# A repeated load taken out, and VectorE's attention steps made smaller and moved inside a pair of blocks, in a fused attention and gated feed-forward kernel

## The chip, the cores and the metric

The kernel runs on one core of a Trainium2 chip. The metric is device time in microseconds (us) of one execution. The time of a kernel is given as the median of its runs. A ratio is the mean time of one kernel's fast runs over that of the other's of the same rounds, so it is not quite the ratio of the medians that stand beside it.

## The reference, cut to what matters

```python
# batch 8, heads 8, seq 576, head_dim 64; all float32
kv  = einsum('bhsd,bhse->bhde', k, v)
out = einsum('bhsd,bhde->bhse', q, kv)
x   = out / sqrt(mean(out*out, -1) + 1e-6) * g_norm      # then (B*S, H*D) = (4608, 512)
gate, val = sigmoid(x @ w_gate), x @ w_val               # 512 -> 1536
return (gate * val) @ w_out                              # 1536 -> 512
```

## The kernel before

The tokens are done in nine chunks of 512. The first chunk is done plainly, beside the loading and converting of the weights and the attention of the first two batches. Chunks 1 to 8 use products with fewer multiplications: a first layer of six pairs of blocks, seven pairs of products each (p1, p6, p2, p7, p5, p4, p3), then a second layer. The attention of batch c + 1 is fed into chunk c, for c from 1 to 6, as a list of small steps. One step is taken from the list after each pair of products. Such a place is called a slot: 42 in the first layer, 28 in the second.

The first two batches, as pairs of heads n = 0 to 7 (NE = 8):

```python
def q_out():                                     # step of pair n
    nc.scalar.copy(out=qT, in_=d["q"])           # after TensorE's transposes of q, line 266
    load_q(n + 4 if n + 4 < NE else n + 2)       # n = 2 asks for q of 6; n = 4 asks for it again
```

The steps of a later batch (NQ = 3; cuts marked):

```python
def kv_copies(i):
    for r in range(NQ):
        nc.vector.tensor_copy(out=kvq[...], in_=kvs[...])
def turn(n):
    for e in range(2):
        nc.vector.transpose(qTs[...], pairs[n]["q"][...])
    load_q(n + 2)
...
fill.extend([turn(n0), turn(n0 + 1)] + [idle] * (0 if early else 5) + [kv_mm, kv_out])   # kv_mm in slot 7
fill.extend([kv_copies(i) for i in range(4)])
fill.extend(two_pairs(n0))     # u_mm (TensorE, reads kvq and qTs), square, sums, root, norms, x_mm, x_out
fill.extend([turn(n0 + 2), turn(n0 + 3)])
fill.extend(two_pairs(n0 + 2))
```

Of the kernel before, what the change touches and what calls it, by code (L numbers as in the profile page):

```python
# [20 lines left out]
def kernel(  # L21
# [11 lines left out]
    nc = tc.nc  # L33

    B, H, S, HD = q.shape
# [4 lines left out]
    NJ = 6  # L40
    NP = S // NJ
# [8 lines left out]
    QB = 32  # L50
    NQ = NP // QB
    QC = QB * NJ
    NC = HD // QB
# [22 lines left out]
    NE = 2 * NHP  # L76
    pairs = {n: {} for n in range(B * NHP)}
# [10 lines left out]
    def load_q(n):  # L88
        if n >= B * NHP:
            return  # L90
        b, h0 = n // NHP, 2 * (n % NHP)
        if n < NE:
            t = first.tile([NP, NJ, 2, HD], FP32, tag="q", name="q")
            for e in range(2):
                nc.sync.dma_start(out=t[:, :, e, :], in_=q[b, h0 + e].rearrange("(p j) d -> p j d", j=NJ))
        else:
            t = sb.tile([NP, 2, NJ * HD], FP32, tag="q", name="q")
            nc.sync.dma_start(out=t, in_=q[b, h0:h0 + 2].rearrange("h (p j) d -> p h (j d)", j=NJ))
        pairs[n]["q"] = t
# [127 lines left out]
    qTs = const.tile([P, 2, 2 * NJ * HD], FP32, name="qTs")  # L227
# [16 lines left out]
    def attention(n, at_ps):  # L244

        b, m = divmod(n, NHP)
        d = {}
        kv = kvs[:, m]

        def kv_mm():  # L250
            d["kv"] = ps = at_ps("kv")
            for j in range(NJ):
                js = slice(HD * j, HD * j + HD)
                for e in range(2):
                    nc.tensor.matmul(ps[HD * e:HD * e + HD, 0, 0:HD], pairs[n]["k"][:, e, js], pairs[n]["v"][:, e, js],  # L255
                                     start=(j == 0), stop=(j == NJ - 1))

        def kv_out():
            nc.vector.tensor_copy(out=kv, in_=d["kv"][:, 0, 0:HD])
            load_kv(n + 4)  # L260

        def q_mm():
            d["q"] = ps = at_ps("q")
            for j in range(NJ):
                c0 = NP * (j % JH)
                nc.tensor.transpose(ps[:, j // JH, c0:c0 + NP], pairs[n]["q"][:, j].rearrange("p e d -> p (e d)"),  # L266
                                    ident[0:NP, 0:NP])

        def q_out():
            d["qT"] = qTs[:, n % 2, 0:S]  # L270
            nc.scalar.copy(out=d["qT"].rearrange("p (i n) -> p i n", i=2), in_=d["q"][:, :, 0:JH * NP])
            load_q(n + 4 if n + 4 < NE else n + 2)

        def u_mm():


            ps = at_ps("u")
            d["u"] = ps[:, :, 0:NU * HD]
            for i in range(2 * NU):
                t0 = min(PH * i, S - PH)  # L280
                r = PH * (i % 2)
                for e in range(2):
                    es = slice(HD * e, HD * e + HD)
                    nc.tensor.matmul(d["u"][r:r + PH, e, HD * (i // 2):HD * (i // 2) + HD],  # L284
                                     d["qT"][es, t0:t0 + PH], kv[es], start=True, stop=True)

        def u_square():
            d["sq"] = sqs[:, NU * P * (n % 2):NU * P * (n % 2 + 1)].rearrange("p (e c) -> p e c", e=2)
            nc.scalar.activation(out=d["sq"], in_=d["u"], func=AF.Square)

        def u_sum():
            d["ms"] = sb.tile([P, 2, NU], FP32, tag="ms", name="ms")
            nc.vector.tensor_reduce(out=d["ms"].rearrange("p e i -> p (e i)"),
                                    in_=d["sq"].rearrange("p e (i d) -> p (e i) d", d=HD), axis=AX.X, op=ALU.add)

        def u_root():
            nc.scalar.activation(out=d["ms"], in_=d["ms"], func=AF.Sqrt, bias=eps, scale=1.0 / HD)

        def u_norm():

            nc.vector.reciprocal(d["ms"], d["ms"])
            d["xn"] = d["sq"].rearrange("p e c -> p (e c)")
            nc.vector.tensor_tensor(out=d["xn"].rearrange("p (i e d) -> p e i d", e=2, d=HD),
                                    in0=d["u"].rearrange("p e (i d) -> p e i d", d=HD),
                                    in1=d["ms"].unsqueeze(3).to_broadcast([P, 2, NU, HD]), op=ALU.mult)

        def x_mm():
            d["x"] = ps = at_ps("x")
            for i in range(NU):
                bank, c0 = divmod(P * i, UX)  # L310
                nc.tensor.transpose(ps[:, bank, c0:c0 + P], d["xn"][:, P * i:P * i + P], ident)  # L311

        def x_out():

            s0 = 0
            while s0 < S:
                c, o = divmod(S * b + s0, G)
                i, r = divmod(s0, UX)
                n_ = min(G - o, (UX if i == 0 else S - UX) - r)
                nc.scalar.activation(out=chunk(c)[:, m, o:o + n_], in_=d["x"][:, i, r:r + n_], func=AF.Copy, scale=g_col)  # L320
                s0 += n_

        return [kv_mm, kv_out, q_mm, q_out, u_mm, u_square, u_sum, u_root, u_norm, x_mm, x_out]


    fill = deque()

    def slot():
        if fill:
            fill.popleft()()  # L330

    def feed(b):

        early = b == 2
# [18 lines left out]
        def kv_out():  # L353
            nc.vector.tensor_copy(out=kvs, in_=d["kv"][:, :, 0:HD])

        def kv_copies(i):
            for r in range(NQ):
                nc.vector.tensor_copy(out=kvq[QB * r:QB * r + QB, :, i], in_=kvs[QB * i:QB * i + QB])  # L358

        def turn(n):  # L360

            for e in range(2):
                w_ = NJ * HD
                nc.vector.transpose(qTs[0:NP, n % 2, w_ * e:w_ * e + w_],
                                    pairs[n]["q"][:, e].rearrange("p (j i c) -> p i j c", i=NC, c=QB))
            load_q(n + 2)

        def two_pairs(n0):

# [26 lines left out]
            def u_sum(i):  # L396
                nc.vector.tensor_reduce(out=ms[:, :, units[i]], in_=by_head(sq)[:, :, units[i]], axis=AX.X, op=ALU.add)
# [4 lines left out]
            def u_norm(i):  # L402
                if i == 0:
                    nc.vector.reciprocal(ms, ms)
                m_ = ms[:, :, units[i]]
                nc.vector.tensor_tensor(out=by_head(sq)[:, :, units[i]], in0=by_head(d["u"])[:, :, units[i]],
                                        in1=m_.unsqueeze(3).to_broadcast([P, NQ, NJ // 2, HD]), op=ALU.mult)
# [7 lines left out]
            def x_out(which):  # L415

                m, s0 = (n0 + which) % NHP, 0
                while s0 < S:
                    c, o = divmod(S * b + s0, G)
                    r, c0 = divmod(s0, QC)  # L420
                    n_ = min(G - o, S - s0) // QC if c0 == 0 else 0
                    w_ = QC if n_ else min(G - o, QC - c0)
                    n_ = max(n_, 1)
                    nc.scalar.activation(out=chunk(c)[:, m, o:o + n_ * w_].rearrange("p (r c) -> p r c", r=n_),
                                         in_=d["x"][:, r:r + n_, QC * which + c0:QC * which + c0 + w_], func=AF.Copy,
                                         scale=g_col)
                    s0 += n_ * w_

            return [u_mm, u_square, lambda: u_sum(0), lambda: u_sum(1), u_root, lambda: u_norm(0), lambda: u_norm(1),
                    idle, x_mm, lambda: x_out(0), lambda: x_out(1)]  # L430

        def idle():
            pass

        n0 = NHP * b
        fill.extend([lambda: turn(n0), lambda: turn(n0 + 1)] + [idle] * (0 if early else 5) + [kv_mm, kv_out])
        fill.extend([lambda i=i: kv_copies(i) for i in range(2 * NC)])
        fill.extend(two_pairs(n0))
        fill.extend([lambda: turn(n0 + 2), lambda: turn(n0 + 3)])
        fill.extend(two_pairs(n0 + 2))  # L440

    def flush():
        while fill:
# [84 lines left out]
    def plain(c, f, ps):  # L528

        blk = Plain(c, f, ps)  # L530
        for at in range(2 * NMT):
            blk.mm(*divmod(at, NMT))
            if at in (0, 2) and late:
# [8 lines left out]
    steps = {"KV": KV, "KVO": KV_OUT, "Q": Q, "QO": Q_OUT, "U": U, "SQ": U_SQUARE, "SUM": U_SUM, "ROOT": U_ROOT,  # L542
             "NORM": U_NORM, "X": X, "XO": X_OUT}
# [16 lines left out]
    for token in order.split():  # L560
        name = token.rstrip("0123456789.")
        n = [int(i) for i in token[len(name):].split(".")]
# [70 lines left out]
    NF2 = NFT // 2  # L633
# [192 lines left out]

    for c in range(1, NG):
        if c + 1 < B:
            feed(c + 1)
        if c == 1:  # L830

            steps = list(fill)
            fill.clear()
            while w2_sums or steps:
                fill.append(w2_sums.popleft() if w2_sums and len(fill) % 7 in (2, 3) else steps.pop(0))
        first_layer_fast(c)
        sums_of(c + 1)
        second_layer_fast(c)
        flush()
# [30 lines left out]
```

## Time and profile before

| | before |
|---|---|
| median of 3 runs | 1116.73 us (1112.47 to 1117.07) |
| span of the profiled run | 1114.4 us |
| TensorE busy | 1091.4 us, 98% |
| VectorE busy | 617.2 us, 55% |
| granted TensorE clock, mean | 0.992 |

The table is where the argument starts: TensorE is busy nearly all the time, so a gain can only come out of its waits and out of stretches in which it runs slower than it could. The prediction shows the views in which both are seen: the table of waits, the chain of work that ended last, and the timeline. In a line of the chain the columns are start, length, and what ran. In a line of the timeline there follow the tile written and read, sizes, the count, and in brackets the idle time before it with what ended it.

### The profile page before, as it was taken

To read this page: it belongs to the slowest core of one execution; us is meant where nothing else is said; L and a number is where in the kernel's file an instruction comes from. 1 tells how busy PE (TensorE), PEld (TensorE's weight loads), DVE (VectorE), ACT (ScalarE), POOL (GpSimd) and SP (SyncE) were. 2 spreads that over 40 slices of the span, in tenths; PEclk is the share of its full clock that TensorE was granted. 3 is DMA by queue.
4 is the path that set the end of the run, shared out by engine and by line. 5 is a ranking of instruction groups with operands and counts; after the bars stand their busy time and mean duration, and the time that the engine had idled before them with its cause. 6 is when DMAs were issued, how large, how long until landed. Compare 5 with 4: busy or idle time off the path is not lost.

```text
span 1114.4 us, 18252 instructions
## 1 busy us (share of the span) xinstructions
PE 1091.4 (98%) x7334; PEld 902.0 (81%) x7334; DVE 617.2 (55%) x1219; ACT 267.3 (24%) x545; POOL 285.3 (26%) x390
## 2 busy tenths in 40 slices
PE   9799999999999999999999999999999999999997
PEld 8444447888888888888888888888888888888886
DVE  4497775773367527771676347642766155515641
ACT  4463322331124101330133013310232011101110
POOL 0000022441234204440334124420344044404500
PEclk9899999999999999999999999999999999999999
DMA  9944712000400022000400040003100000000001
GB/s 266 221 151 151 236 38 60 1 23 19 125 2 22 1 81 65 22 2 19 126 1 23 18 122 7 22 2 107 38 2 1 22 17 1 1 28 11 1 1 38
DMA packets 59657, 58.41 MB, mean 52 GB/s; under 512 B 20916, under 2 KB 53556, under 8 KB 59572
## 3 DMA queue, kind: packets, MB, share of 16 engines
q1 hardware_dynamic: 59412, 57.23, 17.6%
q8 instruction: 59, 0.97, 0.4%
q14 instruction: 26, 0.21, 0.1%
q10 hardware_dynamic: 160, 0.00, 0.0%
HBM read 47.78 MB, written 9.44 MB: 51 GB/s over the span
## 4 chain that ended last, share of the span: by engine, by line
PE 94%; DVE 4%; issue 1%; DMA 1%; SPq 0%; ACT 0%; POOL 0%; DVEq 0%; POOLq 0%
PE mm L669 49%; PE mm L755 26%; PE mm L516 7%; PE mm L613 4%; DVE kvq L358 2%; PE at L388 2%; PE at L344 1%; PE at L413 1%; PE mm L594 1%; PE at L516 1%; DMA q<-in_q_dram 1%; PE two L255 1%; PE two L284 0%; PE two L311 0%; PE two L266 0%
## 5 line engine op out<-in xcount | busy, mean ns | idle before, releaser
L656 POOL TENSOR_TENSOR tw<-gv 128x256 f32<-128x256 f32 x192 | 138.8, 733 | 775.2 <-PE mm L669 612.0
L669 PE MATMUL mm<-xT,gv 128*128 128x256 f32 x768 | 184.8, 384 | 0.0
L669 PE MATMUL mm<-xT,tw 128*128 128x256 f32 x768 | 181.6, 379 | 0.5 <-DVE gv L683 0.5
L669 PE MATMUL mm<-sx,tw 128*128 128x256 f32 x768 | 182.0, 380 | 0.0
L669 PEld LDWEIGHTS mm<-xT,gv 128*128 128x128 f32 x768 | 146.6, 192 | 21.2 <-issue 0.5
L669 PEld LDWEIGHTS mm<-xT,tw 128*128 128x128 f32 x768 | 145.8, 190 | 20.6 <-issue 0.8
L669 PEld LDWEIGHTS mm<-sx,tw 128*128 128x128 f32 x768 | 145.2, 190 | 19.7
L656 POOL TENSOR_TENSOR tw<-gv,tw 128x256 f32<-128x256 f32 x192 | 151.7, 811 | 0.2
L669 PE MATMUL mm<-sx,gv 128*128 128x256 f32 x384 | 91.3, 381 | 0.0
L701 ACT ACTIVATE sg<-sg 128x256 f32<-128x256 f32 x96 | 39.5, 417 | 206.7 <-DVE sg L700 206.3
L755 PE MATMUL mm<-w,s 128*128 128x256 f32 (+1 forms) x408 | 88.3, 367 | 0.0
L755 PE MATMUL mm<-w,gv 128*128 128x256 f32 x384 | 88.1, 379 | 0.0
L755 PE MATMUL mm<-t2w,gv 128*128 128x256 f32 x384 | 88.1, 379 | 0.0
L708 DVE TENSOR_TENSOR gv<-gv,sg 128x512 f32<-128x512 f32 x96 | 88.1, 956 | 0.0
L691 DVE TENSOR_TENSOR gv<-mm,sg 128x256 f32<-128x256 f32 x96 | 40.6, 424 | 81.6 <-PE mm L669 81.6
L677 ACT COPY sg<-mm 128x256 f32<-128x256 f32 x96 | 35.7, 372 | 201.6 <-PE mm L669 183.6
L755 PEld LDWEIGHTS mm<-w,s 128*128 128x128 f32 x408 | 74.1, 190 | 9.4
L755 PEld LDWEIGHTS mm<-w,gv 128*128 128x128 f32 x384 | 72.9, 190 | 9.9
L755 PEld LDWEIGHTS mm<-t2w,gv 128*128 128x128 f32 x384 | 72.9, 190 | 9.9
L669 PEld LDWEIGHTS mm<-sx,gv 128*128 128x128 f32 x384 | 72.5, 190 | 10.0
L516 PE MATMUL mm<-xT,gv 128*128 128x512 f32 x176 | 79.5, 606 | 0.0
L705 DVE TENSOR_TENSOR gv<-mm,gv 128x256 f32<-128x256 f32 x96 | 40.2, 423 | 44.8 <-PE mm L669 44.5
(99 smaller groups left out, 1040.8 us busy)
## 6 DMA issues: line engine op xcount, KB each, us to landing
q<-in_q_dram SPq DMA_DIRECT2D x24, 288.0 KB
st<-in_moe_w_gate_dram SPq DMA_DIRECT2D x12, 512.0 KB
st<-in_moe_w_val_dram SPq DMA_DIRECT2D x12, 512.0 KB
st<-in_moe_w_out_dram SPq DMA_DIRECT2D x12, 512.0 KB
kv<-in_k_dram SPq DMA_DIRECT2D x24, 256.0 KB
kv<-in_v_dram SPq DMA_DIRECT2D x24, 256.0 KB
out_dram<-sg SPq DMA_DIRECT2D x17, 256.0 KB
out_dram<-sg SPq DMA_DIRECT2D x25, 128.0 KB
```

The lines of the kernel that those rows point to most:

```text
L358: nc.vector.tensor_copy(out=kvq[QB * r:QB * r + QB, :, i], in_=kvs[QB * i:QB * i + QB])
L388: nc.tensor.matmul(u[PH * half:PH * half + PH, r, P * s + HD * e:P * s + HD * e + HD], qTs[QB * r:QB * r + QB, (n0 + which) % 2, c:c + PH] ...
L516: nc.tensor.matmul(self.ps[i], w[("wg", "wv")[i], self.f][:, m, :], xT[self.c][:, m, :], start=(m == 0), stop=(m == NMT - 1), skip_group_c ...
L613: nc.tensor.matmul(ps[t], gv[0, f][:, P * t:P * t + P], w["wo", f], start=(f == 0), stop=(f == NFT - 1), skip_group_check=True)
L656: nc.gpsimd.tensor_tensor(out=tw[f, i], in0=b[in0], in1=b[in1] if isinstance(in1, tuple) else tw[f, in1], op=ALU.subtract)
L669: nc.tensor.matmul(ps, wt[:, m, :], xs[:, m, :], start=(new and m == 0), stop=(m == NK - 1), skip_group_check=True)
L677: nc.scalar.copy(out=d["sg"][:, h2], in_=pa)
L691: tt(out=d["h"][:, h2], in0=d["pb"], in1=d["sg"][:, h2], op=ALU.add)
L701: nc.scalar.activation(out=d["sg"][:, h2], in_=d["sg"][:, h2], func=AF.Sigmoid)
L705: tt(out=d["h"][:, h1], in0=d["pc"], in1=d["h"][:, h1], op=ALU.add)
L708: tt(out=d["h"], in0=d["h"], in1=d["sg"], op=ALU.mult)
L755: nc.tensor.matmul(ps, hs(f), ws[:, f, :], start=(new and f == 0), stop=(f == NF2 - 1), skip_group_check=True)
```

## The change

Two things are intended. The second load of q for pairs 6 and 7 is dropped. And VectorE's steps for attention are halved and put only into those slots of a pair of blocks in which VectorE has room. The core of the diff, with cuts marked:

```diff
-            load_q(n + 4 if n + 4 < NE else n + 2)
+            for i in (n + 4,) if n + 4 < NE else (n + 2,) if n + 2 >= NE else ():
+                load_q(i)
...
-        def kv_copies(i):
-            for r in range(NQ):
+        def kv_copies(i, rs):
+            for r in rs:
...
-        fill.extend([lambda: turn(n0), lambda: turn(n0 + 1)] + [idle] * (0 if early else 5) + [kv_mm, kv_out])
-        fill.extend([lambda i=i: kv_copies(i) for i in range(2 * NC)])
-        fill.extend(two_pairs(n0))
-        ...
+        steps = turns_of(n0) + turns_of(n0 + 1)
+        if b > 2:
+            steps += [(PE, idle)] * (7 - len(steps))
+        steps += [(PE, kv_mm), (DVE, kv_out)]
+        for i in range(2 * NC):
+            for rs in ((0, 1), (2,)):
+                steps.append((DVE, lambda i=i, rs=rs: kv_copies(i, rs)))
+        steps += u0 + turns_of(n0 + 2) + x0 + turns_of(n0 + 3) + u1 + [(PE, idle)] * 2 + x1
...
+    def spread(steps, at):
+        n = 0
+        for engine, step in steps:
+            while engine == DVE and n < 7 * NF2 and n % 7 not in at:
+                fill.append(idle)
+                n += 1
+            fill.append(step)
+            n += 1
...
+            spread(steps, (1, 2, 3, 4, 5) if c == 1 else (2, 3, 4, 5))
```

More of the change, by code (lines that the diff above doesn't have):

```diff
@@ L330, in slot @@
             fill.popleft()()
+    PE, DVE, ACT = range(3)
     def feed(b):
@@ L354, in kv_out, with turn @@
             nc.vector.tensor_copy(out=kvs, in_=d["kv"][:, :, 0:HD])
-        def kv_copies(i):
-            for r in range(NQ):
+        def kv_copies(i, rs):
+            for r in rs:
                 nc.vector.tensor_copy(out=kvq[QB * r:QB * r + QB, :, i], in_=kvs[QB * i:QB * i + QB])
-        def turn(n):
-            for e in range(2):
-                w_ = NJ * HD
-                nc.vector.transpose(qTs[0:NP, n % 2, w_ * e:w_ * e + w_],
-                                    pairs[n]["q"][:, e].rearrange("p (j i c) -> p i j c", i=NC, c=QB))
-            load_q(n + 2)
+        def turn(n, e):
+            w_ = NJ * HD
+            nc.vector.transpose(qTs[0:NP, n % 2, w_ * e:w_ * e + w_],
+                                pairs[n]["q"][:, e].rearrange("p (j i c) -> p i j c", i=NC, c=QB))
+            if e == 1:
+                load_q(n + 2)
         def two_pairs(n0):
@@ L427, in x_out, with turns_of, idle @@
                     s0 += n_ * w_
-            return [u_mm, u_square, lambda: u_sum(0), lambda: u_sum(1), u_root, lambda: u_norm(0), lambda: u_norm(1),
-                    idle, x_mm, lambda: x_out(0), lambda: x_out(1)]
-        def idle():
-            pass
-        n0 = NHP * b
-        fill.extend([lambda: turn(n0), lambda: turn(n0 + 1)] + [idle] * (0 if early else 5) + [kv_mm, kv_out])
-        fill.extend([lambda i=i: kv_copies(i) for i in range(2 * NC)])
-        fill.extend(two_pairs(n0))
-        fill.extend([lambda: turn(n0 + 2), lambda: turn(n0 + 3)])
-        fill.extend(two_pairs(n0 + 2))
+            return ([(PE, u_mm), (ACT, u_square), (DVE, lambda: u_sum(0)), (DVE, lambda: u_sum(1)), (ACT, u_root),
+                     (DVE, lambda: u_norm(0)), (DVE, lambda: u_norm(1))],
+                    [(PE, x_mm), (ACT, lambda: x_out(0)), (ACT, lambda: x_out(1))])
+        def turns_of(n):
+            return [(DVE, lambda n=n, e=e: turn(n, e)) for e in range(2)]
+        n0 = NHP * b
+        u0, x0 = two_pairs(n0)
+        u1, x1 = two_pairs(n0 + 2)
+        steps = turns_of(n0) + turns_of(n0 + 1)
[6 more added lines that the diff above has]
+        steps += u0 + turns_of(n0 + 2) + x0 + turns_of(n0 + 3) + u1 + [(PE, idle)] * 2 + x1
+        return steps
+    def idle():
+        pass
+    def spread(steps, at):
[6 more added lines that the diff above has]
+            n += 1
     def flush():
@@ L828 @@
         if c + 1 < B:
-            feed(c + 1)
-        if c == 1:
-            steps = list(fill)
-            fill.clear()
-            while w2_sums or steps:
-                fill.append(w2_sums.popleft() if w2_sums and len(fill) % 7 in (2, 3) else steps.pop(0))
+            steps = feed(c + 1)
+            if c == 1:
+                i = 5
+                while w2_sums:
+                    steps.insert(i, (DVE, w2_sums.popleft()))
+                    i += 3
+            spread(steps, (1, 2, 3, 4, 5) if c == 1 else (2, 3, 4, 5))
         first_layer_fast(c)
```

## The prediction

> **What bounds the kernel now.** I read the page's busy shares first, then TensorE's waits, then the chain that ended last in order of time, then the timeline of the two places that those views name.
>
> ```profile
> PE 1091.4 (98%) x7334; PEld 902.0 (81%) x7334; DVE 617.2 (55%) x1219; ACT 267.3 (24%) x545; POOL 285.3 (26%) x390
> PE two L266 <- DMA q<-in_q_dram: 8.2, 1, 8.2
> PE at L388 <- DVE kvq L358: 4.6, 10, 0.5
> PE at L388 <- DVE qTs L364: 1.0, 1, 1.0
> PE mm L669 <- DVE gv L683: 0.5, 1, 0.5
> ```
>
> TensorE is 98% busy, so only what makes it wait, or run slower than it could, can be won. It waits once for q (8.2 us) and some dozen times for VectorE (about 6 us). That table counts only bare idle time, so I looked at both places more closely. The chain around the wait for q (start, length, what):
>
> ```profile
> 37.99 1.44 SPq L95
> 39.47 5.84 DMA q<-in_q_dram
> 45.44 1.19 PE two L266 x6
> 46.64 1.76 PE mm L516 x2
> 48.40 1.07 PE two L311 x5
> 49.46 3.74 PE mm L516 x6
> 53.20 0.74 PE two L284 x40
> ```
>
> The load of q issued at 37.99 is the second one for pair 6: step 4 asks for q of n + 2 = 6, although step 2 had asked for n + 4 = 6. The pair's transposes (L266) take the later copy. After the wait TensorE is also slow: 0.88 us for one 128x512 matmul (two records in 1.76) where 58.37 us for 136 records, later in the same chain, is 0.43 a record, 0.86 a pair. Six transposes take 1.19 us against 0.65 for the same six at 56.35, five take 1.07 against 0.55 at 64.47. The granted clock between 45.4 and 53.1 is 0.59.
>
> TensorE in the first layer of the third of the eight chunks that are done with the cheaper products (waits in brackets):
>
> ```profile
> 438.55 0.68 PE L388 MATMUL at<-kvq,qTs 32*64 32x64 f32 x36
> 439.75 0.33 PE L388 MATMUL at<-kvq,qTs 32*64 32x64 f32 x4 [0.51 <-DVE kvq L358]
> 440.49 1.64 PE L388 MATMUL at<-kvq,qTs 32*64 32x64 f32 x104 [0.41 <-DVE kvq L358]
> 442.06 1.99 PE L669 MATMUL mm<-xT,gv 128*128 128x256 f32 x8
> ```
>
> From 438.55 to 442.06 is 3.51 us; the same 144 matmuls without a wait, later in this chunk (465.76 in the chain), take 1.73. VectorE shows why:
>
> ```profile
> 433.94 1.32 DVE L358 COPY kvq<-kvs 32x256 f32<-32x256 f32 x3
> 436.08 2.20 DVE L358 COPY kvq<-kvs 32x256 f32<-32x256 f32 x3
> ```
>
> Three copies stand in each of four slots. The first three take 0.88 us, later ones 1.3 to 2.2, because a copy takes 0.28 us alone and up to 0.73 while GpSimd's sums (L656, from 434.39) run.
>
> [...] the slow spell here lasts about 6 us. [...]
>
> **The change, part 1: the double load.** Two loads of 288 KB go. Pair 6 then uses the copy issued at 26.38. Loads are issued on one queue, so I count bytes: seven pairs of k, v (590 KB each), seven of q (295 KB) and two weight units (1.05 MB) are 8.29 MB. The first slice moved 266 GB/s over 27.9 us, 7.4 MB; the other 0.88 MB at 284 GB/s take 3.1 us. Estimate: landed at 31, or 33 with the 2 us by which the same count is early for the second q. TensorE is ready for it at 37.2. So the wait of 8.2 us goes. With it goes the slow spell: 45.44 to 53.13 is 7.7 us for work that takes 4.6 at full clock (0.56 + 0.9 + 0.55 + 2.58), so 3.1. What could come in its place: pair 7's k, v, q and the third weight unit. Their counts give 39 to 40 and 37 us with the same lag, and they are wanted at about 44, 45 and 40. VectorE's and ScalarE's conversions were held by the same wait (VectorE idle 8.35 us behind L266) and move with it. Sum of part 1: **-11.3 us**.
>
> **Part 2: the steps amid a pair of blocks.** A slot is 8 matmuls of 128x256 at 0.216, 1.73 us. Seven slots are a pair of blocks. VectorE's own work is two operations of 0.42 after five of the seven products, and after the last another 2.1 + 1.5 us (gate products and sums), about 4.1 us until it is free. So slots 0, 1 and 6 have no room, slot 2 all of it, slots 3 to 5 some 0.9 each. Before, steps went one per slot wherever they fell, whole. The four copy slots asked for 0.88, 1.32, 2.20, 1.66, and the matmuls that read them stood right behind. After, steps stand in slots 2 to 5 only (1 to 5 in the first of these chunks), halved: transpose 0.53, copies two and one (0.58, 0.29; 0.73 if GpSimd runs), sums 0.74, norms 0.76. All but the last fit their slots. From the second chunk on, the reading matmuls come in slot 25 instead of 13, one slot of 1.73 us after the last copy of 0.29; the second four heads' matmuls fall in the second layer, where VectorE is busy 10.2 of 36.2 us. Total work on TensorE stays the same.
>
> What TensorE loses now, against 1.73 us for each such group and 0.1 us of switching:
>
> - chunk 1: 0.81 (wait for gv) + 0.35 + 1.50 = 2.66
> - chunk 2: 1.83 + 1.59 (half clock for 7 matmuls after the wait) = 3.42
> - chunk 3: 1.77
> - chunk 4: 2.37 + 0.97 (half clock again) = 3.34
> - chunk 5: 1.77 + 0.16 + 0.20 = 2.13
> - chunk 6: 1.77 + 0.42 = 2.19
>
> The sum is 15.5. As a check: the six stages take 501.2 us together in the chain; one without attention takes 72.52, and attention adds 2.40 + 2 x 1.73 + 2 x 0.98 and five switches of 0.1, so 80.85 each without waits, which leaves 16.0. I expect about 15 back. The one place that is tight: the second group in the second layer needs the last transposes. VectorE is free 4.1 us after the second layer starts (as 966.65 - 962.5 shows in a chunk without attention), plus two of 0.53 is 5.2. The group starts after 24 matmuls, 5.2 us, but reads the last half only 0.87 us later. Margin 0.8 us, so at most a few tenths are lost.
>
> Sum: 1116.7 - 11.3 - 15 = 1090.4.
>
> **Rivals.** (a) The early stage is bound by loads or conversions, so the wait only moves: the queues are full there (284 GB/s), which speaks for it. Against it, stages of the same mix before 36 us ran without a gap, and the counts above leave 3 to 5 us. It would leave 5 of the 11 us: 1096. (b) VectorE falls behind elsewhere (37 steps in the first chunk with 12 weight sums among them; transposes at the start of the second layer), and half of part 2 comes back: 1098. [...] Against it: its work is 59 of 83.5 us in that chunk, and each slot was counted to fit. (c) The attention of the second four heads now ends late in the second layer, and the next chunk's input sums wait: 2 us in each of six chunks, 1102. Against it: the sums stand in slots 58 to 61 of 70, some 10 us before their use; in the first of these chunks in 64 to 67, the closest case.
>
> **Range and chances.** All working gives 1089.9, with no losses; I allow half a microsecond. What is left to win is bounded (TensorE's work is fixed), so the low end is 1087 (run to run the kernel before moved 4.6 us). The high end, 1098, holds (a) or (b). Two per cent is 1094.4, and I give 0.84 to being below it, 0.15 to within, 0.01 to slower.
>
> **What would show it.** In the new profile: TensorE waits for no q; L266's eight groups follow without a gap and the granted clock of the second slice is full; the wait for kvq is under 0.5 us in all; every group of 144 attention matmuls takes 1.7 to 1.8 us; the span is near 1088. Wrong: a new wait of TensorE before 65 us (part 1), for qTs at the start of the second layer or for sx at the start of a chunk (part 2), or half clock after any of these.

## More of the kernel before

Output tiles and gate tiles come from one pool of four:

```python
def sg_tile():
    return sb.tile([P, G], FP32, tag="sg", name="sg", bufs=4)

def p1():
    product(pa, ..., True)
    d["sg"] = sg_tile()
    nc.scalar.copy(out=d["sg"][:, h2], in_=pa)       # ScalarE
...
def p2():
    product(d["pa"], ..., False)                     # adds to pa: must wait until that copy has read it
...
# end of the second half of the second layer
store(c, 2 + g, o2)
if g == 1:
    load_late(c + 2)         # 12 loads of k and v for a later chunk, 2.3 MB
...
if not last:
    store(c, g, o1)          # the last store of the chunk, behind those loads
```

## The result, and the profile after

| | before | after |
|---|---|---|
| median of 4 runs each | 1115.09 us | 1098.83 us (1096.87 to 1102.08) |
| ratio of fast runs | | 0.9858 (95%: 0.9824 to 0.9893) |
| span of the profiled run | 1114.4 | 1100.3 |

The change is faster by 1.4%. The prediction was 1090.4 us in a range of 1087 to 1098, so the result lies 0.8 us outside the range, and a gain of over 2%, to which it gave 0.84, did not come.

TensorE's waits in the profile after, in all, how many, the longest:

```profile
PE mm L693 <- ACT sg L701: 6.0, 4, 2.7
PE two L255 <- DMA v<-in_v_dram: 2.1, 1, 2.1
```

No line names q, kvq or qTs any more: each wait that the prediction wanted gone is gone. Two new ones stand there. (L693 is the line that was L669, L701 was L677.)

The early stage, from the chain after:

```profile
40.93 0.64 PE two L266 x6
41.57 0.89 PE mm L540 x2
...
57.40 58.37 PE mm L540 x136
```

The transposes of pair 6 run at full pace (0.64 us for six, where they took 1.19 before). The long run of 136 matmuls starts at 57.40, where it started at 65.02 before: 7.6 us earlier and not 11.3. The wait of 2.1 us for v, early on, and a half-clock spell after it (granted clock 0.61 from 20.0 to 24.4) took the rest. Whether they belong to the change is tested below.

The attention matmuls of chunk 4, TensorE's timeline after:

```profile
566.02 1.89 PE L693 MATMUL mm<-sx,tw 128*128 128x256 f32 x8
567.85 1.80 PE L391 MATMUL at<-kvq,qTs 32*64 32x64 f32 x144
569.57 1.99 PE L693 MATMUL mm<-xT,tw 128*128 128x256 f32 x8
```

The group of 144 now takes 569.57 - 567.85 = 1.72 us without a gap (in this chunk it took 561.67 - 557.57 = 4.1 before, with the start of a half-clock spell in it, granted clock 0.68 from 559.5 to 564.8; 3.5 in the chunk that the prediction shows), and so do all twelve such groups. Three lines of VectorE's copies for it, in the same chunk:

```profile
554.59 0.28 DVE L361 COPY kvq<-kvs 32x256 f32<-32x256 f32 x1
556.32 1.19 DVE L361 COPY kvq<-kvs 32x256 f32<-32x256 f32 x2
566.68 0.29 DVE L361 COPY kvq<-kvs 32x256 f32<-32x256 f32 x1
```

The last copy is done at 566.97, 0.9 us before its readers start. So both parts did what they were meant to do, and yet from the start of the 136 matmuls to the start of chunk 7 only 825.14 - 818.73 = 6.4 us were won (890.16 - 65.02 before, 876.13 - 57.40 after), where 15 were expected. The missing time is in the new wait for ScalarE. The chain after, at the start of chunk 4, shows where that comes from:

```profile
516.24 1.74 PE mm L693 x8
...
518.32 7.61 DMA kv<-in_v_dram
...
525.95 8.55 DMA out_dram<-sg
...
534.60 0.38 ACT sg L701
...
535.02 1.13 PE mm L693 x4
536.16 3.54 PE at L347 x64
```

It is to be read downwards: the second part of the last store of the chunk before is issued at 525.95, 9.9 us after this chunk began at 516.08; it takes 8.55 us; its tile is then free for ScalarE's copy after p1 of the second pair of blocks; and only after the copy may TensorE run p2 (535.02). Then the k by v products (L347) run at 3.54 us where they take 2.02 at full clock, as in chunk 3 (the granted clock from 535.0 to 539.7 is 0.64, from 416.3 to 418.3 it is 1.00).

The line of the load of v above the store must not be read as its cause: the store waits for it for 0.2 us only. What makes the issue late is its place, behind the twelve loads that are issued from 514.77 to 524.92. What makes the store long is mostly not the loads. In the trace's DMA records, told apart by the size of the packets, its 128 packets of 2 KB run from 526.4 to 534.2, while the last packet of the k and v loads ends at 527.6. The store before chunk 2, to rows of the output that lie in another order, moves its 128 packets in 1.6 us. Why this one is so slow was not tested.

TensorE there, after and before:

```profile
531.62 1.03 PE L693 MATMUL mm<-xT,gv 128*128 128x256 f32 x4
535.02 1.13 PE L693 MATMUL mm<-xT,gv 128*128 128x256 f32 x4 [2.38 <-ACT sg L701]
536.09 3.61 PE L347 MATMUL at<-kv 128*64 128x64 f32 x64
```

```profile
542.75 1.89 PE L669 MATMUL mm<-xT,gv 128*128 128x256 f32 x8
544.57 2.09 PE L344 MATMUL at<-kv 128*64 128x64 f32 x64
546.59 0.46 PE L350 MATMUL at<-kv 64*64 64x64 f32 x16
546.98 1.99 PE L669 MATMUL mm<-sx,tw 128*128 128x256 f32 x8
548.81 1.92 PE L669 MATMUL mm<-xT,gv 128*128 128x256 f32 x8
```

and ScalarE's copies in the kernel before, same chunk:

```profile
543.82 0.37 ACT L677 COPY sg<-mm 128x256 f32<-128x256 f32 x1 [1.72 <-PE mm L669]
549.18 0.37 ACT L677 COPY sg<-mm 128x256 f32<-128x256 f32 x1 [4.99 <-DMA out_dram<-sg]
```

The late store was there before the change: ScalarE waited 4.99 us for it, 18.5 us into the chunk. But TensorE had the k by v products to do (2.4 us) between p1 and p6, so the second product of the p2 pair, which needs that copy, began at about 549.7 (548.81 and four of 0.216). The copy ended at 549.55. The wait was hidden with 0.1 us to spare, and no view of TensorE's waits could show it. The change moved the 2.4 us behind p2.

The loss per chunk: the stretch of 80 matmuls between the start of a chunk and its k by v products takes 17.36 us in chunk 2, where the store is issued 6.3 us into the chunk and is short, and 18.01, 20.01, 20.35 and 18.12 in chunks 3 to 6, together 7.05 more. With 1.5 us for the half clock in chunk 4 that is 8.6 us, nearly all of what is missing from the 15.

### The profile page after: what moved, and what is told of

Same layout as the page of the kernel before. It is cut to its first block, busy times and chain, and to the rows that moved or that the text cites. A ratio compares the mean times of both kernels' runs of the same rounds, so it can differ in the third digit from the quotient of the medians.

```text
span 1100.3 us, 18225 instructions
## 1 busy us (share of the span) xinstructions
PE 1083.6 (98%) x7334; PEld 897.9 (82%) x7334; DVE 619.7 (56%) x1219; ACT 267.5 (24%) x545; POOL 289.9 (26%) x390
## 4 chain that ended last, share of the span: by engine, by line
PE 93%; DMA 5%; SPq 1%; ACT 0%; issue 0%; DVE 0%; ACTq 0%
PE mm L693 49%; PE mm L779 26%; PE mm L540 7%; PE mm L637 4%; DMA out_dram<-sg 2%; PE at L391 2%; DMA kv<-in_v_dram 1%; PE at L347 1%; PE at L416 1%; DMA v<-in_v_dram 1%; DMA kv<-in_k_dram 1%; PE at L540 1%; PE two L255 0%; PE two L312 0%; PE two L285 0%; PE two L266 0%
## 5 line engine op out<-in xcount | busy, mean ns | idle before, releaser
L693 PE MATMUL mm<-xT,gv 128*128 128x256 f32 x768 | 182.5, 380 | 6.0 <-ACT sg L701 6.0
L693 PE MATMUL mm<-xT,tw 128*128 128x256 f32 x768 | 182.7, 380 | 0.2 <-issue 0.2
L693 PE MATMUL mm<-sx,tw 128*128 128x256 f32 x768 | 181.4, 379 | 0.0
L693 PEld LDWEIGHTS mm<-xT,gv 128*128 128x128 f32 x768 | 145.6, 190 | 27.6 <-ACT sg L701 7.6
L693 PEld LDWEIGHTS mm<-sx,tw 128*128 128x128 f32 x768 | 145.9, 190 | 19.8
L693 PEld LDWEIGHTS mm<-xT,tw 128*128 128x128 f32 x768 | 145.0, 190 | 20.6 <-issue 0.7
L680 POOL TENSOR_TENSOR tw<-gv,tw 128x256 f32<-128x256 f32 x192 | 155.8, 832 | 0.0
L693 PE MATMUL mm<-sx,gv 128*128 128x256 f32 x384 | 90.9, 380 | 0.0
L732 DVE TENSOR_TENSOR gv<-gv,sg 128x512 f32<-128x512 f32 x96 | 90.7, 983 | 0.0
L693 PEld LDWEIGHTS mm<-sx,gv 128*128 128x128 f32 x384 | 72.4, 190 | 9.7
L701 ACT COPY sg<-mm 128x256 f32<-128x256 f32 x96 | 35.8, 373 | 178.6 <-PE mm L693 165.1
L711 ACT ACTIVATE sg<-mm 128x256 f32<-128x256 f32 x96 | 36.9, 384 | 111.0 <-PE mm L693 111.0
```

What stands on the lines that cost most here:

```text
L680: nc.gpsimd.tensor_tensor(out=tw[f, i], in0=b[in0], in1=b[in1] if isinstance(in1, tuple) else tw[f, in1], op=ALU.subtract)
L693: nc.tensor.matmul(ps, wt[:, m, :], xs[:, m, :], start=(new and m == 0), stop=(m == NK - 1), skip_group_check=True)
L711: nc.scalar.activation(out=d["sg"][:, h1], in_=d["pa"], func=AF.Sigmoid)
L732: tt(out=d["h"], in0=d["h"], in1=d["sg"], op=ALU.mult)
```

## The experiments

Theory: the loss is that of the move of `kv_mm` from slot 7 to slot 9, which lays open the wait for the last store's tile. Rivals: the smaller steps win less than was counted; part 1 wins less; or the traffic of the loads delays things whatever the order. All runs gave right results. The table has, from the chain of each profiled run, the start of the 136 matmuls, the stretch from there to chunk 7, and the span; the rest of the span is 224.1 to 224.3 us in every one of them. The kernel before had a median of 1114.07 us in the rounds of the first four runs and 1115.23 in those of the other four, which ran on another chip; medians are best compared within a half.

| kernel | start of 136 | stretch | span | median | ratio to before |
|---|---|---|---|---|---|
| before | 65.02 | 825.14 | 1114.4 | | |
| after, first profile | 57.40 | 818.73 | 1100.3 | 1098.83 | 0.9858 |
| load_only | 53.73 | 821.79 | 1099.7 | 1104.25 | 0.9904 |
| steps_only | 65.48 | 816.84 | 1106.6 | 1110.13 | 0.9967 |
| kv_slot7 | 53.62 | 810.22 | 1088.1 | 1089.83 | 0.9785 |
| store_first | 52.70 | 811.06 | 1087.9 | 1089.54 | 0.9777 |
| after_again | 53.45 | 819.21 | 1096.8 | 1099.32 | 0.9852 |
| five_sg | 53.23 | 810.81 | 1088.2 | 1091.12 | 0.9778 |
| kv_slot8 | 52.93 | 810.50 | 1087.6 | 1089.80 | 0.9767 |
| before_kv9 | 65.82 | 851.51 | 1141.6 | 1141.53 | 1.0230 |

**load_only**: the load alone, on the kernel before.

```diff
-            load_q(n + 4 if n + 4 < NE else n + 2)
+            for i in (n + 4,) if n + 4 < NE else (n + 2,) if n + 2 >= NE else ():
+                load_q(i)
```

> The kernel before with the second q load removed and nothing else. Theory: the wait of 8.2 us for q and the half clock after it (3.1 us) go, the stages with attention stay as they were (groups of 144 attention matmuls of 3.5 us in chunks 2 to 6, about 15.5 us lost): ratio to before 0.990, about 1104.5 us. Rival: the early stage is bound by loads, another wait before 65 us takes some of it (as the profiled run of the change showed, 2.1 us for v and a slow spell): ratio 0.993 to 0.995.

The 136 matmuls start 65.02 - 53.73 = 11.3 us earlier, exactly what part 1 said, and the ratio is 0.9904 (0.9888 to 0.9920), about 10.7 us. No wait for v of any size is seen. The stretch is 3.3 us shorter than in the first profile of the kernel before, although nothing in it differs: the five groups of 144 matmuls take 3.5 us each in chunks 2 to 6 in this run too, but the half-clock spells that followed two of them before are missing (the next 64 matmuls take 14.01 us here, in chunks 2 and 4 alike; before, they took 15.60 in chunk 2 and 14.98 in chunk 4). So those 2.6 us of the prediction's 15.5 come in some runs and not in others. The profiled run is the fastest of the five, 1101.47 us; the others took 1103.63 to 1105.20 at a mean clock of 0.995 to 0.996 in place of 0.998. It is likely, though no profile shows it, that they had such spells, so 821.79 is a favourable stretch.

**steps_only**: the changed kernel with the second load back.

```diff
-            for i in (n + 4,) if n + 4 < NE else (n + 2,) if n + 2 >= NE else ():
-                load_q(i)
+            load_q(n + 4 if n + 4 < NE else n + 2)
```

> The changed kernel with the second q load put back. Theory: the waits for VectorE in the attention stages go (-15.5 us), but in chunks 3 to 6 the second product of the second pair of blocks waits 0.6 to 3 us for the output tile that the last store of the chunk before still holds, 8.9 us in all with half clock after two of them: ratio 0.994, about 1109 us. Rival: the steps' own gain is smaller than counted, or the loss is the early stage's: then this run shows no such waits and still stands near 0.994, or it stands at 0.986.

TensorE's waits:

```profile
PE two L266 <- DMA q<-in_q_dram: 9.8, 1, 9.8
PE mm L692 <- ACT sg L700: 5.4, 4, 2.6
```

The wait for q is back, and so is the wait for ScalarE's copy, without any wait for VectorE. Part 2 as it stands is worth little: the ratio is 0.9967 (0.9949 to 0.9985), about 3.7 us, somewhat less than the 0.994 expected.

**kv_slot7**: the changed kernel with the k by v products where they were.

```diff
-            steps += [(PE, idle)] * (7 - len(steps))
+            steps += [(PE, idle)] * (5 - len(steps))
```

> The changed kernel with the k by v products back in slot 7 (between the first and the second product of the second pair of blocks) where the kernel before had them, in place of slot 9 (after the second use of the tile's bank). Theory: the store lands as late as now (the ScalarE copy still starts at +16.5 to +18.9 us of the chunk), but 2.4 us of k by v products stand before the matmul that waits, so TensorE's wait for ScalarE falls from 6.0 to under 0.7 us and the half clock after it goes: 8 to 8.9 us less than the changed kernel, ratio to before 0.977 to 0.979. Rival: the late store is a matter of VectorE's steps or of q's loads: nothing changes, 0.986.

TensorE's waits for ScalarE's copy are gone from the table, the ratio is 0.9785 and the median 1089.83 us. ScalarE's copy still waits for the store until 16.7 to 18.7 us of chunks 3 to 6, as predicted: the store has not become faster, the wait is hidden again.

**store_first**: the changed kernel with the loads behind the last store.

```diff
-            if g == 1:
-                load_late(c + 2)
...
             if not last:
                 store(c, g, o1)
+            if g == 1:
+                load_late(c + 2)
```

> The changed kernel with the loads of the next k and v issued after the last store of the chunk in place of before it. Theory: the last store is issued about +1 us into the chunk in place of +9 to +11, its tile is free before +13, the ScalarE copy no longer waits for it and TensorE not for the copy: 8 to 9 us less, ratio 0.977 to 0.979, unless k and v come later than slot 9 wants them (15.6 us into the chunk). Rival: the store is slow because the transfers are, not because of its place in the queue: the copy still waits, 0.984 to 0.986.

The same time by the other end of the chain. ScalarE's copies in chunk 4:

```profile
524.42 0.37 ACT L701 COPY sg<-mm 128x256 f32<-128x256 f32 x1 [1.71 <-PE mm L693]
525.32 0.37 ACT L701 COPY sg<-mm 128x256 f32<-128x256 f32 x1 [0.54 <-PE mm L693]
```

The second copy waits for the matmul before it and not for a store. The k and v loads, now last, were still in time for slot 9. With 1089.54 us, and four runs within 0.3 us, this version beats both kernels: ratio 0.9777 (0.9761 to 0.9792).

**after_again**: the changed kernel, unaltered, for a second profile.

> The changed kernel once more, unchanged. Theory: the wait of 2.1 us for v at 16.7 us of the first profile and the half clock after it belong to that run and not to the change (the kernel with the load alone had none): a second profile is without it, the long run of 136 matmuls starts at 53.5 us in place of 57.4, the waits for ScalarE's copy are there again (5 to 6 us), and the median is 1097 to 1099. Rival: the change makes it, then it is there again.

The wait for v is 0.5 us in this run where the first profile had 2.1, the 136 matmuls start at 53.45, and the waits for ScalarE's copy are 6.0 us in four places again. A wait of 1.7 us for v at the same line (L255) also stands in the profile of before_kv9 below, which has neither part of the change. So the late v varies from run to run and is not the change's, and the run of the first profile is the slowest of the changed kernel's first four (1102.08 us); the wait for the copy is the change's. The median, 1099.32, is just above the expected band.

**five_sg**: the changed kernel with a fifth tile.

```diff
-        return sb.tile([P, G], FP32, tag="sg", name="sg", bufs=4)
+        return sb.tile([P, G], FP32, tag="sg", name="sg", bufs=5)
```

> The changed kernel with five tiles for outputs and gates in place of four, and the queue as it was. Theory: the last store is still issued at +9 to +11 us of the chunk and lands as late, but the copy in the second pair of blocks gets another tile, which has long been stored, so neither ScalarE nor TensorE waits: 1089 to 1090.5 us. Rival: what delays is the traffic of the k and v loads itself and not the tile: the waits stay, 1097 or more.

The last store is issued as late as before (9.1 to 11.3 us into chunks 3 to 6), yet both copies start at 13.2 and 14.0 us in each chunk and TensorE waits for neither. SyncE's issue and ScalarE's copies in chunk 5, which starts at 628.74:

```profile
640.06 0.62 SPq L493 DMA_DIRECT2D out_dram<-sg  x1
641.93 0.37 ACT L701 COPY sg<-mm 128x256 f32<-128x256 f32 x1 [1.76 <-PE mm L693]
642.75 0.37 ACT L701 COPY sg<-mm 128x256 f32<-128x256 f32 x1 [0.45 <-PE mm L693]
```

The ratio is 0.9778; the median of 1091.12 is 0.6 us above the band. So what was waited for is the tile that the store holds, and not the traffic.

**kv_slot8**: the k by v products between p6 and p2.

```diff
-            steps += [(PE, idle)] * (7 - len(steps))
+            steps += [(PE, idle)] * (6 - len(steps))
```

> The changed kernel with the k by v products in slot 8, after the first two products of the second pair of blocks and right before the one that waited. Theory: what counts is 2.4 us of other work ahead of the matmul that needs the copy, not how early k by v is done: as with slot 7, 1089 to 1091 us, TensorE's wait for ScalarE under 0.7 us. Rival: it is the earlier VectorE copy that helps: then slot 8 stands between, about 1094.

```profile
526.59 2.09 PE L347 MATMUL at<-kv 128*64 128x64 f32 x64
528.61 0.46 PE L353 MATMUL at<-kv 64*64 64x64 f32 x16
529.00 1.99 PE L693 MATMUL mm<-xT,gv 128*128 128x256 f32 x8
```

```profile
528.95 0.37 ACT L701 COPY sg<-mm 128x256 f32<-128x256 f32 x1 [4.47 <-DMA out_dram<-sg]
```

TensorE's lines (first) and ScalarE's (second) in chunk 4: the copy starts 4.47 us late, at 528.95, while TensorE does the k by v products, and p2 at 529.00 needs it for its second half only, at 529.86. TensorE's wait for the copy is 0.2 us in all, the median 1089.80 us, the ratio 0.9767. One slot decides: in slot 8 the products hide the wait, in slot 9 they come after it.

**before_kv9**: the move alone, on the kernel before.

```diff
-        fill.extend([...] + [idle] * (0 if early else 5) + [kv_mm, kv_out])
+        fill.extend([...] + [idle] * (0 if early else 7) + [kv_mm, kv_out])
```

> The kernel before with nothing but the k by v products two slots later (seven idle steps in place of five). Theory: TensorE waits for ScalarE's copy in chunks 3 to 6 as in the changed kernel, 5 to 6 us of it and 8 to 9 with the half clock; the copies of VectorE move too, which may give back or cost 2 to 4 us: ratio 1.004 to 1.010. Rival: the wait needs the smaller steps: no wait for ScalarE's copy here, ratio 0.997 to 1.002.

```profile
PE at L388 <- DVE kvq L358: 9.1, 5, 1.8
...
PE mm L669 <- ACT sg L677: 5.2, 4, 2.5
PE mm L669 <- DVE gv L705: 3.6, 5, 0.7
```

The wait for ScalarE's copy appears in four places, 5.2 us, with no other part of the change in the kernel: the move alone makes it. The size was missed widely, though: the ratio is 1.023. The whole copies now fall on the border between two pairs of blocks, where VectorE has its 4.1 us of other work, and the waits for kvq double. That part of the loss has nothing to do with the store; it shows what whole steps on the border cost. The stretch is 26.4 us longer than in the kernel before. The bare waits account for some 14 of it (4.5 more for kvq, 5.2 for the copy, 3.1 more for gv, 1.6 for sqs). The rest is about what half clock takes, as an estimate from the mean clocks: 0.018 x 1141.6 less 0.008 x 1114.4 is 11.6 us.

## Why the prediction was wrong, point by point

- **What bounds the kernel**: right. Every gain and loss that was followed here is a wait of TensorE or a half-clock spell after one.
- **Part 1, -11.3**: right. The load alone moved the 136 matmuls by 11.3 us, and nothing took the place of the wait there. Its small sums hold to 0.1 us, although the six transposes are entered with 0.56 where its own text has 0.65. Rival (a) fell. The half clock after the wait of 8.2 us came and went with it: before, the granted clock was 0.59 from 45.4 to 53.1; in load_only the same six transposes take 0.64 us in place of 1.19, and the two matmuls behind them 0.89 in place of 1.76.
- **Part 2, the waits removed**: right in mechanism. The waits for kvq, qTs and gv are gone, the tight place at the start of the second layer cost nothing, rival (b) fell, and the input sums of rival (c) were in time. Its size was nearly right: with the wait for the store hidden or gone, the medians of the same rounds differ from load_only's by 1104.25 - 1089.83 = 14.4 us (kv_slot7) and 14.7 us (store_first). By the profiles the stretch shrinks by 825.14 - 810.50 = 14.6 us against the kernel before, whose profile had the half-clock spells, and by 11.3 against load_only's, which had not. 15.5 took those spells as certain.
- **The step that failed** is the sum of part 2, "I expect about 15 back", with its ground "Total work on TensorE stays the same". The total does, the order does not. The working followed VectorE's steps from slot to slot and named slot 25 for their readers, but passed over the k by v products, which go from slot 7 to 9. There they no longer stand ahead of p2, which waits for a copy, which waits for a tile, which waits for a store. In place of "no losses" the runs showed 8.6 us in the first profile, and 1098.83 to 1099.32 us against 1089.80 with the products one slot earlier.
- **The rivals**: none of the three named it. The list of what would show it wrong named waits for qTs and sx, not one for ScalarE. The trace of the kernel before did hold the sign: ScalarE idle 3 to 5 us for a store, just before a copy that TensorE reads next, in four chunks.
- With the products in slot 7, 8 or the store first, the time is 1089.5 to 1089.8 us, half a microsecond from the 1089.9 that the working gave without losses; five tiles give 1091.1. The error is this one term. That nearness is one of the end, not of the gain: the working took the losses of one profiled run, 1116.26 us, off a median of 1116.73, while the later medians of the kernel before are 1114.07 and 1115.23. Against these the gains are 24.1 to 25.4 us and not 26.8.

## What to carry to other kernels

A step that is moved takes its cover with it. For each step that a change shifts, look at the matmul that used to stand behind it, and at how much time was left between that matmul and what it needs; an idle time of an engine "that is not the bottleneck" may be hidden by tenths of a microsecond only (here ScalarE's, by 0.1 us). And a store that frees a tile should not stand in a queue behind loads that are wanted much later (here its place ahead of them took the ratio from 0.9858 to 0.9777).

## When half clock came, and when not

- The spell after the idle time of 8.2 us lasted some 6 us from TensorE's next matmul on, at 45.44 (granted clock 0.50 from 41.4 to 51.7). Half clock also followed much shorter waits: after 2.4 us in the changed kernel (k by v products at 3.54 in place of 2.02 us), and in the kernel before, in chunk 2, after a group of small matmuls with two gaps of 0.5 and 0.4 us (seven of the next matmuls at about 0.43 in place of 0.216 us; granted clock 0.54 from 321.5 to 325.0). With equal gaps it came in one profile and not in the next: after 2.38 us in chunk 4 of the changed kernel's first profile, and not after 2.40 us in chunk 4 of its second, where the k by v products take 2.02 us; what decides is left open.
